# A new written-out order, with new engines and buffers, for every step of a fused recurrence and feed-forward kernel

## The chip, the cores and the metric

The kernel runs on one core of a Trainium2 chip. The core has a matmul engine (TensorE, PE in the profile), three engines for elementwise work (VectorE = DVE, ScalarE = ACT, GpSimd = POOL), a queue engine (SyncE = SP) that issues most DMAs, and 16 DMA engines. Matmul results go to PSUM, which this kernel divides into eight banks; all else lies in SBUF. The metric is the device time of one execution in microseconds (us).

## What is computed

A gated linear recurrence (4 batches, 8 heads, 768 tokens, 48 channels per head) gives 3072 rows of 384 numbers, and these pass through a feed-forward layer with the activation h cos(h):

```python
f = 1.0 / (1.0 + np.exp(-f_logit))
for t in range(S):
    state = f[:, :, t, :, None] * state + np.einsum('bhd,bhe->bhde', k[:, :, t], v[:, :, t])
    y[:, :, t] = np.einsum('bhd,bhde->bhe', q[:, :, t], state)
# x is y as (3072, 384)
h = x @ w_in          # 384 -> 2048
g = h * np.cos(h)
out = g @ w_out       # 2048 -> 384
```

## The kernel before

The tokens are cut into twelve pairs (0 to 11) of two chunks of 128 tokens; three pairs make one batch. A pair is the recurrence's unit of work, and a feed-forward unit with the same number takes the pair's 256 rows. `describe` builds a graph of some 900 named steps. A step's name is its kind, the pair or unit, and behind a dot the half (0 or 1), the quarter, or both. In the order of the data the kinds are:

- `f`, `k`, `q`, `v`: loads of a pair's operands (L336). Pairs 0 and 1 load f, k, q and v in halves of 192 KB; the others load 384 KB at once. Only `f0.0` is issued by ScalarE, the rest by SP.
- `ex`, `ln` (and `fx`, `fy`): exponentials and logarithms of the gates on ScalarE (L372, L378, L392, L389); `ad` adds two of them on GpSimd (L410). `cum` sums them along the tokens with matmuls (L424 to L456), and `eb`, `ei` take the exponentials of the sums (L472, L476, L481).
- `qa`, `ka`, `qm`, `km`: q and k multiplied with the decays, 1 us each on GpSimd (L386, L396, L492, L503, L507); `vb` casts v (L520 for pairs 0 and 1, where it also reads a mask; a plain cast elsewhere).
- `tq`, `tk`, `qkt`: q and k turned. Pairs 0 to 3 turn them with matmuls (L569, L575) and copy the result out of PSUM (`qkt`). Pairs 4 to 11 use one transposing DMA per half (`tq`, L558), issued by SP, and have no `tk` and no `qkt`.
- `sc`, `am`, `vs`, `vt`: scores of a chunk (L595), their masking on VectorE (L599), and v in the layout that the products need.
- `ps`, `sj`, `st`, `sz`: the state's outer products (L616, L626), the old state added by a matmul (L641, pairs 0 and 1) or on VectorE (L647), and the decay of the new state (L652).
- `y`, `yi`, `xe`: the outputs of a pair (L680) and their copy out of PSUM. This is the x of the feed-forward unit.
- `w0.i`, `w1.i`: the four quarters of w_in and w_out, 768 KB each in f32, loaded into g buffers (L320); `wc` casts each to bf16.
- `h`, `co`, `g`: the first product (L728), the cosine on ScalarE (L733), the product on VectorE (L710). `h2.31` is unit 2, quarter 3, second half; quarter j of `h` needs quarter j of w_in.
- `o`, `ot`, `out`: the second product of 128 rows (L744), `o5.3` being row block 5 (unit 2) and quarter 3, which needs quarter 3 of w_out; the copy out of PSUM and the store (L755). The last unit's `ot` and `out` are cut in two.
- `zf`: a matmul on zeros (L302) that computes nothing; `z...` with other names clear paddings of buffers; `cqp`, `cqi`, `cqs` build masks; `ctl` does nothing but ask for ScalarE's table of exponentials.

What is run when is a text, `ORDER`: one word per step, in one sequence for all engines. The letter behind the colon is the engine (T TensorE, S ScalarE, V VectorE, G GpSimd, Y SP), the digits are the buffer or PSUM bank that the step's result is given. `emit` walks it and emits each step on its engine, so each engine, and SP's queue of DMAs, runs its own words strictly in the text's order. The tile framework adds the waits: a step waits for its operands, and a step that writes a buffer waits for all who still read it. A load whose buffer is in use thus holds SP, and all loads, transposes and stores behind it. ScalarE has one table for exponentials and one for the cosine; going from one to the other costs a table load (L786, or at L733). PSUM banks are shared by all kinds, so a matmul step may also wait for the copy that empties its bank.

So the text alone sets the order of the work; the kernel has no planner, costs or due times of its own.

Of the kernel before, what the change touches and what calls it, by code (L numbers as in the profile page):

```python
# [866 lines left out]
```

## Time and profile before

| | |
|---|---|
| runs | 180.32, 181.04, 181.69 us; median 181.04 |
| the profiled execution | 181.73 us, of which the span from the first to the last instruction is 179.9 us |
| TensorE busy | 170.9 us (95% of the span), granted clock 0.997 |
| VectorE, ScalarE, GpSimd busy | 132.5, 132.2, 97.5 us |
| DMA | 34.46 MB, 192 GB/s over the span |
| zeros (L302) | 27 steps, 8.5 us of recorded matmul time |

Busy time is time in which at least one instruction of the engine runs. TensorE's ends are modelled, since matmuls overlap. An engine's busy share is an average over stages: at the start the DMAs set the pace, later TensorE does. "Idle before" is the time an engine stood still ahead of an instruction, with what ended the wait.

### The profile page before, as it was taken

How to read it: one execution, taken by the hardware profiler on the slowest of the kernel's cores; microseconds unless marked ns; L12 is line 12 of the kernel's file. 1: busy time of each engine (PE TensorE's matmuls, PEld its weight loads, DVE VectorE, ACT ScalarE, POOL GpSimd, SP SyncE). 2: the span in 40 equal slices, each digit the busy share in tenths (PEclk: the TensorE clock that was granted, in tenths of full speed). 3: DMA queues.
4: the chain of work that ended last, by engine and by line, in shares of the span. 5: the costliest groups of instructions: out<-in, count | busy, mean ns of one | idle time of the engine just before them, and what ended most of it. 6: DMA issues, size and time to landing. Idle time of an engine off the chain costs nothing.

```text
span 179.9 us, 5963 instructions
## 1 busy us (share of the span) xinstructions
PE 170.9 (95%) x2543; PEld 124.4 (69%) x2545; DVE 132.5 (74%) x210; ACT 132.2 (73%) x181; POOL 97.5 (54%) x119
## 2 busy tenths in 40 slices
...
GB/s 126 306 300 267 333 353 206 348 374 272 247 264 242 195 239 205 284 212 190 242 213 275 271 264 203 224 231 58 4 0 56 206 4 46 175 5 0 0 91 131
DMA packets 70330, 34.46 MB, mean 192 GB/s; under 512 B 59296, under 2 KB 68768, under 8 KB 70304
## 3 DMA queue, kind: packets, MB, share of 16 engines
...
q14 instruction: 6, 0.05, 0.1%
...
## 4 chain that ended last, share of the span: by engine, by line
PE 74%; DMA 14%; SPq 3%; POOL 3%; DVE 2%; ACT 1%; issue 1%; DVEq 0%; POOLq 0%
PE ps L744 32%; PE ps L728 30%; PE ps L680 5%; DMA q<-in_q_dram 4%; DMA g<-in_moe_w_in_dram 4%; SPq L336 3%; PE ps L595 3%; DMA v<-in_v_dram 3%; DMA qkt<-qk 3%; PE ps L626 2%; DVE g L710 1%; POOL qk L507 1%; POOL w_in_bf L197 1%; PE ps L424 1%; POOL qk L503 1%; DVE vq L520 1%
## 5 line engine op out<-in xcount | busy, mean ns | idle before, releaser
L710 DVE TENSOR_TENSOR g<-ps,co 128x1024 bf16<-128x1024 f32 x48 | 58.0, 1221 | 22.6 <-ACT co L733 20.0
L744 PE MATMUL ps<-w_out_bf,g 128*128 128x384 bf16 x384 | 68.4, 326 | 0.0
L728 PE MATMUL ps<-x,w_in_bf 128*128 128x256 bf16 x576 | 67.4, 273 | 0.6 <-POOL w_in_bf L197 0.4
L733 ACT ACTIVATE co<-ps,halfpi 128x1024 bf16<-128x1024 f32 x48 | 52.7, 1115 | 19.1 <-PE ps L728 18.5
L728 PEld LDWEIGHTS <-w_in_bf 128*128 128x128 bf16 x576 | 55.5, 98 | 9.5 <-POOL w_in_bf L197 1.0
L744 PEld LDWEIGHTS <-g 128*128 128x128 bf16 x384 | 35.9, 98 | 21.7
L599 DVE TENSOR_TENSOR am<-ps,pmask 128x1024 bf16<-128x1024 f32 x24 | 28.6, 1217 | 3.9 <-PE ps L595 3.6
L507 POOL TENSOR_TENSOR qk<-k,bi 128x384 bf16<-128x384 f32 x16 | 15.8, 1000 | 7.6 <-issue 7.0
L507 POOL TENSOR_TENSOR qk<-q,b 128x384 bf16<-128x384 f32 x16 | 15.8, 1002 | 0.5
L197 ACT COPY ot<-ps 128x384 f32<-128x384 f32 (+1 forms) x12 | 4.9, 422 | 12.7 <-PE ps L744 12.7
L372 ACT ACTIVATE f<-f 128x768 f32<-128x768 f32 (+1 forms) x14 | 10.4, 751 | 4.4 <-DMA f<-in_f_logit_dram 4.3
L197 POOL COPY vt<-vb 64x384 bf16<-64x384 bf16 x25 | 12.5, 503 | 1.2
L410 POOL TENSOR_TENSOR sp<-ls 128x384 bf16<-128x384 f32 x8 | 8.0, 1000 | 7.3 <-ACT ls L378 6.4
L647 DVE TENSOR_TENSOR ps<-ps,sz 128x192 f32<-128x192 f32 x26 | 9.4, 361 | 0.9 <-PE ps L626 0.5
L197 DVE CAST x<-ps 128x384 bf16<-128x384 f32 x12 | 6.5, 552 | 4.5 <-PE ps L680 4.5
L197 DVE COPY ot<-ps 128x384 f32<-128x384 f32 x14 | 7.7, 554 | 2.8 <-PE ps L744 2.6
L302 PE MATMUL ps<-zero 128*128 128x512 bf16 x25 | 8.5, 464 | 1.4 <-DVE zero L203 1.2
L595 PE MATMUL ps<-qkt 48*64 48x128 bf16 x384 | 8.3, 220 | 1.5 <-DMA qkt<-qk 1.4
L492 POOL TENSOR_TENSOR qk<-q,bq 128x384 bf16<-128x384 f32 x3 | 3.0, 1008 | 11.6 <-DMA q<-in_q_dram 11.4
L386 POOL TENSOR_TENSOR q<-f,q 128x384 f32<-128x384 f32 x8 | 8.0, 1001 | 2.2 <-DMA q<-in_q_dram 2.1
L652 DVE TENSOR_TENSOR sz<-ps,b 128x192 bf16<-128x192 f32 x26 | 8.4, 350 | 0.8 <-PE ps L626 0.6
L786 ACT ACT_TABLE_LOAD x6 | 7.7, 1283 | 1.6 <-PEq L851 1.5
...
## 6 DMA issues: line engine op xcount, KB each, us to landing
...
```

The source lines that it names most:

```text
L197: (nc.scalar.copy if e == "ACT" else eng(e).tensor_copy)(out=o, in_=i)
L302: G.step(f"zf{i}", ("PE",), lambda e, dump=dump: nc.tensor.matmul(dump.ap, lhsT=zero[:, 0:128], rhs=zero, start=True, stop=True), writes=[ ...
L372: nc.scalar.activation(out=flat(t.ap), in_=flat(t.ap), func=AF.Exp, scale=-1.0)
L507: G.step(f"{nm}{n}.{u}", ("POOL", "DVE") if cut else ("POOL",), lambda e, u=u, j=j, src=src, dec=dec: eng(e).tensor_mul(out=qkp[u][j].ap[: ...
L595: nc.tensor.matmul(o[64 * h:64 * h + 64, r, 2 * a + g, :].rearrange("p (e n) -> p e n", e=2), lhsT=qkv(u)[s, 1, a, g, h, :], rhs=qkv(u)[s, ...
L599: G.step(f"am{n}.{u}", ("DVE",), lambda e, u=u, sc=sc: nc.vector.tensor_mul(out=am[u].ap.rearrange("p r b n -> p (r b) n"), in0=sc.ap.rear ...
L647: G.step(f"st{n}.{g}{r}", ("DVE",), lambda e, r=r, view=view, S0=S0: nc.vector.tensor_add(out=view(), in0=view(), in1=S0.ap[:, :, r, :]), ...
L680: nc.tensor.matmul(py[g].ap[32 * c:32 * c + 32, C * m:C * m + C], start=(py[g].first and (g, c) not in begun), stop=(py[g].final and left[ ...
L710: nc.vector.tensor_mul(out=o.rearrange("p b (n e) -> p b n e", e=2), in0=ph.ap.rearrange("p (b e n) -> p b n e", e=2, n=64), in1=co.ap.rea ...
L728: nc.tensor.matmul(ph.ap[:, i * T:(i + 1) * T].rearrange("p (g t) -> p g t", t=C), lhsT=w_in_bf[:, kk, f0:f0 + 128], rhs=xa[:, :, kk, :], ...
L733: G.step(f"co{m}.{j}", ("ACT",), lambda e, ph=ph, co=co: nc.scalar.activation(out=co.ap, in_=ph.ap, func=AF.Sin, bias=halfpi), reads=[ph], ...
L744: nc.tensor.matmul(po.ap[:, 0:DM], lhsT=gT.ap[:, j, i * C:(i + 1) * C], rhs=w_out_bf[:, j, :], start=(po.first and j == 4 * s), stop=(po.f ...
```

## The change

The program's steps stay the same, but for seven more matmuls on zeros. `ORDER` is replaced as a whole: each engine's sequence, the engine of a step where it may have several, and the buffers and banks. At the start:

- On SP's queue f3 comes right behind f0, then k0.1 and v0, then f1.0, k0.0 and q0; f2 comes behind v1.1. All of pairs 0 and 1 and f2 and f3 still go ahead of the first weight, which is now w0.0.
- The second half of pair 0 (`.1`) goes first through `ex`, `ln`, `cum`, `eb`, `ei`, `km`, and its first half follows. `km0.1` moves from VectorE to GpSimd, `cqp` too.
- The score steps of pair 1 go ahead of the first `h`; `ps1.0` and `sj1.0` go behind `h0.01`, `y1` and `yi1` behind `h0.11`.
- The weights' quarters come as w0.0, w0.1, w0.2, w0.3, w1.0, w1.3, w1.1, w1.2, with k2, q2, k3, v2, q3, f4 and v3 between them.

Later on, all `qkt` copies are on VectorE (four were on ScalarE), `vb8` and `vb10` are on GpSimd (they were on ScalarE), the order of SP's loads, transposes and stores is another one throughout, and of the last tile's two halves one is copied on ScalarE and the other on VectorE. `ctl` moves from the middle to the last microseconds.

```diff
-ZEROS = 27
+ZEROS = 34
 ORDER = """
-f0.0:S1 f0.1:Y cqp:V zsp.2:V zqk.1:G cqs:V zvt.2:G ex0.0:S cqi:V ex0.1:S ln0.0:S2 f2:Y3 v0.0:Y1
-v0.1:Y vb0.1:V0 k0.0:Y1 vb0.0:V f1.0:Y0 ln0.1:S ex2:S zf0:T4 zf1:T4 zf2:T4 zf3:T4 zf4:T4 zf5:T4
-zf6:T4 zf7:T4 zf8:T4 zf9:T4 zf10:T4 cum0.0:T7 k0.1:Y ei0.0:S cum0.1:T6 ei0.1:S km0.0:V1 km0.1:V
-f3:Y2 q0.1:Y1 ln2:S2 zf11:T4 zf12:T4 zf13:T4 zf14:T4 zf15:T4 zf16:T4 zf17:T4 zf18:T4 cum2:T2 q0.0:Y
-f1.1:Y v1.0:Y1 k1.1:Y2 ex1.0:S q1.0:Y0 ps0.0:T0,1 eb0.0:S0 eb0.1:S ln1.0:S2 ps0.1:T eb2:S1 sz0.01:V0
-ei2:S ex3:S ex1.1:S k1.0:Y vs0:T4 vt0.0:V2 sz0.00:V cum1.0:T6 ln1.1:S eb1.0:S2 tk0.1:T7 qm0.1:V
-qm0.0:G v1.1:Y tk0.0:T0 q1.1:Y w0.1:Y3 ei1.0:S sj0.1:T sz0.11:V2 zqk.2:G w0.0:Y4 tq0.1:T qkt0.1:V2
-vt0.1:S qm1.0:G2 zf19:T2 zf20:T2 zf21:T2 tq0.0:T sz0.10:V sc0.1:T2 zf22:T7 cum1.1:T1 ln3:S2
-qkt0.0:V4 yi0:T0 am0.1:V0 sc0.0:T6 w0.2:Y1 am0.0:V1 eb1.1:S zf23:T5 tq1.0:T4 vb1.1:V0 cum3:T2
-ei1.1:S km1.0:G tk1.0:T eb3:S0 w0.3:Y0 qm1.1:G sj1.0:T6 y0:T7 vb1.0:V ei3:S xe0.1:V0 km1.1:G xe0.0:V
-zf24:T5 zf25:T5 ps1.0:T1 zf26:T5 ps1.1:T sz1.01:V0 vs1:T2 qkt1.0:S0 tq1.1:T0 vt1.1:S2 wc0.1:G
-sz1.00:V tk1.1:T wc0.0:G sj1.1:T vt1.0:V qkt1.1:V4 h0.11:T4 sc1.0:T2 sc1.1:T6 k3:Y1 h0.10:T
-sz1.10:V3 sz1.11:V k2:Y0 h0.01:T0 zsp.1:V am1.0:V2 co0.1:S0 h0.00:T co0.0:S1 yi1:T2,3 am1.1:V0
-wc0.2:G y1:T xe1.1:S2 h0.20:T6 g0.1:V3 xe1.0:S zvt.1:V wc0.3:G km3.1:G1 h0.21:T co0.2:S0 h1.11:T2
-h1.10:T g0.0:V g0.2:V h1.01:T0 q2:Y2 w1.2:Y4 h1.00:T km2.1:G2 h1.20:T4 q3:Y1 h1.21:T co1.1:S3
-km2.0:G g1.1:V0 co1.0:S2 g1.0:V h0.31:T2 w1.0:Y1 co1.2:S3 h1.30:T6 tk2.0:T1 qm2.1:G wc1.2:S tq2.1:T0
-h0.30:T co0.3:S0 g1.2:V qm2.0:G tk2.1:T km3.0:G qm3.0:G tq2.0:T qkt2.1:V1 tk3.0:T5 qkt2.0:S4 h1.31:T
-tk3.1:T4 o0.2:T0 tq3.0:T qm3.1:V tq3.1:T w1.1:Y2 g0.3:V qkt3.0:S0 o3.2:T1 o1.2:T2 o2.2:T3 co1.3:S2
-qkt3.1:S3 g1.3:V w1.3:Y4 wc1.0:G o1.0:T o2.0:T sc3.1:T4 wc1.3:G v3:Y1 f4:Y1 v2:Y0 sc2.0:T6 am2.0:V2
-wc1.1:S o3.0:T am3.1:V0 o0.1:T o3.1:T o3.3:T ot3:V2 vb3:G2 ex4:S vt3.0:S2 vt3.3:G f5:Y0 sc3.0:T4
-am3.0:V1 ln4:S0 q4:Y0 sc2.1:T6 am2.1:V3 vt3.1:G vt3.2:G vb2:G0 fx4:S ad4:G2 o2.1:T o2.3:T o0.0:T
-ps3.0:T4,1 ps3.1:T k4:Y0 ps2.1:T5 ot2:V1 fy4:S ps2.0:T sz3.01:V0 vt2.0:S1 o0.3:T sz3.00:V o1.3:T
...
-ex7:S qm5.0:G ln7:S1 ad6:G1 am4.0:V1 tq5.0:Y4 v8:Y0 am4.1:V3 ps5.0:T st5.00:V k7:Y2 o6.1:T7 o5.0:T
-ot4:S2 out4:Y o5.1:T vt4.3:G ot5:V3 st5.01:V cum6:T0 sz5.01:V1 ad7:G2 fx6:S vt5.0:G1 vt5.3:S eb6:S2
-sz5.00:V vt5.2:S ei6:S0 o6.2:T y4:T2,3 yi4:T xe4.1:V1 xe4.0:S fx7:S vt5.1:G sc5.1:T4 sc5.0:T0
-cum7:T6 h4.00:T2 am5.0:V2 zqk.0:V h4.01:T q6:Y1 o6.3:T v7:Y2 am5.1:V3 h3.01:T0 eb7:S1 ei7:S1 ka6:G
-km6.0:G2 zvt.0:V yi5:T4,5 vb6:G1 y5:T zsp.0:G co4.0:S2 g4.0:V3 h3.00:T q7:Y0 xe5.1:S0 ka7:G
-ps6.0:T5,6 fy6:S km6.1:G ps6.1:T sz6.00:V1 f9:Y0 qa6:G h4.20:T2 qm6.0:G sz6.01:V xe5.0:V h4.21:T
-fy7:S co3.0:S2 vt6.0:S2 g3.0:V h4.31:T4 h4.30:T co4.2:S1 co4.3:S0 h5.11:T0 qm6.1:G tq6.0:Y2 f8:Y2
-st6.10:V st6.11:V out5:Y h5.10:T g4.2:V qa7:G o6.0:T h4.10:T2 sz6.11:V2 g4.3:V h4.11:T vb8:S0
-co5.1:S1 km7.0:G1 qm7.0:G g5.1:V0 ot6:S2 vt6.3:G sz6.10:V h5.21:T4 co4.1:S2 tq6.1:Y4 g4.1:V h5.20:T
-o7.2:T7 vb7:G2 k8:Y1 co5.2:S1 tq7.0:Y0 g5.2:V qm7.1:G km7.1:G ex8:S ex9:S ln9:S0 fy9:S ad9:G2 fx9:S
-o7.3:T o7.0:T o7.1:T ot7:V3 tq7.1:Y1 vt7.0:G0 ln8:S1 ps7.0:T0,6 ps7.1:T vt8.0:G1 st7.00:V vt7.2:G
-sc6.1:T4 vt6.1:S k9:Y0 sc6.0:T2 fx8:S o9.3:T1 o9.0:T o8.3:T7 am6.1:V1 o8.0:T st7.01:V out7:Y vt7.1:S
-sc7.1:T4 am6.0:V3 f10:Y1 sc7.0:T2 o9.1:T q9:Y1 am7.1:V2 o9.2:T ot9:V3 sz7.01:V0 v11:Y2 out9:Y
...
-h11.30:T6 out19:Y h11.10:T out15:Y h11.31:T co10.0:S3 g10.0:V o23.0:T3 o21.2:T o20.0:T co11.3:S0
-g11.3:V o20.2:T ot20:S0 o22.0:T2 co11.1:S2 out20:Y o23.3:T o21.3:T o22.3:T g11.1:V o21.0:T ot21:V0
-o23.1:T out18:Y o23.2:T ot23.0:S3 out21:Y o22.1:T out23.0:Y ot23.1:S out23.1:S o22.2:T ot22.1:S2
-out22.1:Y ot22.0:S out22.0:S
+f0.0:S2 f0.1:Y f3:Y0 cqi:V zvt.0:V cqp:G k0.1:Y1 zsp.2:V ex0.1:S v0.0:Y1 zqk.2:V cqs:V v0.1:Y
+f1.0:Y1 zsp.1:G ln0.1:S2 ex0.0:S zf0:T5 zf1:T5 zf2:T5 zf3:T5 zf4:T5 zf5:T5 zf6:T5 zf7:T5 zf8:T5
+zf9:T5 zf10:T5 zf11:T5 cum0.1:T7 eb0.1:S2 ei0.1:S km0.1:G2 ln0.0:S zf12:T5 zf13:T5 zf14:T5 zf15:T5
+zf16:T5 zf17:T5 zf18:T5 zf19:T5 cum0.0:T6 ex3:S vb0.1:V1 ei0.0:S k0.0:Y tk0.1:T7 ex1.0:S eb0.0:S
+q0.1:Y1 vb0.0:V zf20:T5 zf21:T5 zf22:T5 zf23:T5 zf24:T5 vs0:T2 ln1.0:S2 ln3:S1 km0.0:V q0.0:Y
+ps0.1:T0,1 f1.1:Y qm0.1:V v1.1:Y1 vt0.0:S0 f2:Y3 k1.0:Y1 ps0.0:T qm0.0:G vt0.1:V ex1.1:S ln1.1:S
+q1.0:Y0 tk0.0:T6 cum1.0:T4 sz0.00:V3 v1.0:Y ei1.0:S sz0.01:V zqk.1:G tq0.1:T k1.1:Y eb1.0:S0 zf25:T2
+zf26:T2 tq0.0:T sj0.1:T qkt0.1:V3 qkt0.0:V1 zf27:T0 zf28:T0 cum1.1:T3 km1.0:G1 q1.1:Y sz0.11:V0
+w0.0:Y0 sz0.10:V sc0.0:T6 yi0:T2 w0.1:Y1 am0.0:V1 sc0.1:T4 am0.1:V2 ex2:S ln2:S2 ei1.1:S k2:Y0
+qm1.0:G cum3:T0 eb3:S2 km1.1:G vb1.1:V1 cum2:T6 eb1.1:S qm1.1:G w0.2:Y2 tk1.0:T5 tq1.0:T qkt1.0:V4
+eb2:S1 y0:T4 vb1.0:V q2:Y2 wc0.0:G xe0.0:V3 ei3:S wc0.1:G zf29:T3 zf30:T3 zf31:T3 tk1.1:T5 w0.3:Y3
+xe0.1:S tq1.1:T ei2:S zf32:T3 ps1.1:T0,1 vs1:T2 qkt1.1:V2 vt1.1:V0 vt1.0:S zf33:T4 sc1.0:T6 sc1.1:T4
+h0.00:T2 am1.1:V3 h0.01:T am1.0:V0 co0.0:S3 ps1.0:T sj1.0:T sz1.00:V3 wc0.2:G h0.11:T4 w1.0:Y0 k3:Y2
+km2.0:G2 y1:T6,7 sz1.01:V yi1:T sj1.1:T w1.3:Y1 xe1.1:V2 h0.10:T g0.0:V4 km2.1:G xe1.0:S h1.11:T6
+h1.10:T qm2.1:G co0.1:S0 sz1.11:V3 h1.00:T2 co1.1:S2 h1.01:T g0.1:V h1.20:T4 tk2.1:T0 g1.1:V2
+h1.21:T tq2.1:T h0.21:T6 sz1.10:V wc0.3:G qm2.0:G co1.0:S3 co1.2:S0 g1.0:V h0.20:T h1.31:T2 g1.2:V
+qkt2.1:V4 v2:Y0 co0.2:S1 q3:Y2 h1.30:T wc1.0:G h0.31:T4 co1.3:S3 tk2.0:T1 g0.2:V w1.1:Y3 h0.30:T
+km3.0:G1 sc2.1:T6 g1.3:V o2.0:T0 tq2.0:T am2.1:V1 qkt2.0:V0 co0.3:S2 km3.1:G o0.0:T3 f4:Y0 o3.0:T2
+o1.0:T7 vb2:G0 g0.3:V vt2.1:G0 wc1.3:S vt2.0:S o3.3:T ps2.0:T6 sc2.0:T4 vt2.2:S am2.0:V3 v3:Y2
+w1.2:Y0 ps2.1:T qm3.0:G vt2.3:S o1.3:T ex4:S ln4:S1 fy4:S qm3.1:G st2.00:V st2.01:V sz2.00:V0
+wc1.1:G vb3:G2 f5:Y1 tk3.1:T1 o0.3:T sz2.01:V o2.3:T tq3.1:T ad4:G1 tq3.0:T4 fx4:S qkt3.1:V2 tk3.0:T
+qkt3.0:V1 o0.1:T y2:T6,1 yi2:T sc3.0:T4 xe2.1:S1 xe2.0:S q4:Y2 k4:Y1 k5:Y2 o3.1:T am3.0:V0 o2.1:T
+ps3.1:T6,1 ps3.0:T sz3.01:V0 vt3.0:G0 sc3.1:T4 zvt.2:G wc1.2:S o1.1:T sz3.00:V cum4:T6 ex5:S vt3.1:G
+ln5:S1 fx5:S fy5:S v4:Y2 o3.2:T ot3:V1 o0.2:T eb4:S0 am3.1:V3 ot0:V0 vt3.3:G o1.2:T vt3.2:G ot1:V2
+o2.2:T ei4:S2 yi3:T4 q5:Y1 ot2:V3 y3:T5 xe3.1:V0 xe3.0:S ad5:G2 cum5:T3 qa4:G qm4.0:G1 f6:Y3
+h2.10:T6 st3.10:V st3.11:V eb5:S2 sz3.11:V2 sz3.10:V h2.11:T ei5:S0 h2.20:T4 co2.1:S0 h3.11:T2
+g2.1:V2 h2.21:T ka4:G h3.10:T km4.0:G co2.2:S1 g2.2:V h3.20:T0 qm4.1:G f7:Y0 out3:Y h3.21:T vb4:G0
+co3.1:S2 co3.2:S0 tq4.0:Y0 h2.01:T6 h2.00:T co2.0:S3 g3.1:V0 h2.30:T4 ka5:G g3.2:V h2.31:T h3.31:T2
+h3.30:T o5.2:T0 km4.1:G tq4.1:Y4 g2.0:V o4.0:T6 co2.3:S1 g2.3:V ps4.0:T7,1 qa5:G sc4.0:T4 co3.3:S0
+v5:Y0 qm5.0:G2 ex6:S ps4.1:T out2:Y km5.0:G qm5.1:G g3.3:V st4.00:V ln6:S0 fy6:S st4.01:V tq5.0:Y3
+o4.3:T f8:Y2 km5.1:G vt4.2:G0 sz4.01:V3 sz4.00:V o4.2:T am4.0:V3 ex7:S ln7:S1 vb5:G1 o4.1:T o5.3:T
+tq5.1:Y2 ot4:S3 o5.1:T st4.10:V o5.0:T sc4.1:T4 v6:Y2 k6:Y1 sc5.0:T2 vt4.3:G fx7:S vt5.0:G2 ad6:G1
+vt5.1:S o6.2:T7 vt5.2:G st4.11:V sz4.10:V0 sz4.11:V am4.1:V1 vt4.0:S o6.1:T q6:Y0 ex8:S k7:Y2
+vt4.1:G ad7:G2 q7:Y1 cum6:T1 ei6:S2 eb6:S1 am5.0:V0 ot5:V1 yi4:T5,4 y4:T xe4.0:V2 ps5.0:T6 vt5.3:G
+ps5.1:T st5.00:V sc5.1:T2 cum7:T0 xe4.1:V o6.3:T fx6:S ei7:S1 h4.01:T4 am5.1:V3 h4.00:T eb7:S0
+out4:Y h3.00:T0 v7:Y0 st5.01:V sz5.00:V2 vb6:G0 co4.0:S2 ka6:G v9:Y1 y5:T2,3 km6.1:G2 sz5.01:V
+out1:Y yi5:T xe5.1:S1 km6.0:G qa6:G f9:Y1 ka7:G h3.01:T ps6.1:T3,6 ps6.0:T fy7:S g4.0:V1 h4.21:T4
+qm6.1:G tq6.1:Y3 h4.20:T xe5.0:V qa7:G sz6.00:V3 sz6.01:V h4.30:T2 km7.0:G1 co3.0:S1 qm7.1:G g3.0:V
+co4.2:S2 g4.2:V km7.1:G h4.31:T h4.10:T0 h4.11:T vb7:G2 st6.10:V st6.11:V co4.3:S0 g4.3:V co4.1:S1
+g4.1:V vt6.0:G2 vt7.3:G0 o6.0:T h5.20:T4 h5.21:T h5.10:T2 qm7.0:G vt6.1:S zsp.0:G co5.2:S0 vt6.3:G
+sz6.10:V1 h5.11:T co5.1:S3 g5.2:V2 ex9:S ln9:S0 o9.2:T0 qm6.0:G f10:Y3 o9.3:T o9.1:T ot6:V2 o7.2:T5
+fy9:S tq7.1:Y1 vt6.2:G out6:Y tq7.0:Y4 g5.1:V tq6.0:Y0 o7.0:T ad9:G2 ps7.0:T3,1 vt7.2:S ps7.1:T
+sz6.11:V sc6.1:T6 k9:Y2 o9.0:T o7.1:T ot9:S3 st7.00:V st7.01:V q9:Y2 ln8:S1 ad8:G0 sz7.00:V2
+am6.1:V0 o7.3:T sz7.01:V st7.10:V cum9:T0 o8.1:T4 ot7:S2 eb9:S1 sc7.1:T6 ei9:S2 sc7.0:T2 out9:Y
+vt7.1:G am7.1:V1 fx8:S qa9:G qm9.0:G2 vt7.0:S o8.0:T v10:Y0 fx9:S vb9:G0 cum8:T5 ei8:S0 o8.2:T
+sc6.0:T6 q8:Y0 f11:Y0 o8.3:T am7.0:V3 eb8:S2 am6.0:V2 ka9:G vb10:G2 qm9.1:G yi6:T2 ot8:S3 y7:T3,0
+yi7:T zqk.0:G st7.11:V sz7.11:V2 k11:Y0 y6:T5 k8:Y1 fy8:S out7:Y sz7.10:V xe6.1:V2 h5.00:T6 xe7.1:V0
+h5.01:T out8:Y vt9.1:G0 km9.0:G tq9.0:Y0 ex10:S xe7.0:S h5.31:T0 xe6.0:V co5.0:S1 g5.0:V h7.20:T2
...
+y11:T5,4 yi11:T xe11.1:S2 sc10.1:T6 tq10.0:Y4 sc10.0:T2 vt10.1:S vt10.0:G o18.3:T1 o19.3:T xe11.0:V
+h11.20:T4 o18.0:T am10.0:V2 o17.3:T2 o17.0:T h11.21:T co11.2:S3 am10.1:V0 o17.1:T yi10:T6,7 y10:T
+xe10.0:V3 out16:Y xe10.1:S o19.1:T o17.2:T h10.31:T6 ot17:V3 h10.30:T g11.2:V2 ot19:V0 h10.21:T2
+co10.3:S2 h10.20:T h10.00:T4 out19:Y h10.01:T o18.1:T o18.2:T g10.3:V0 out17:Y h11.30:T6 co10.2:S2
+h11.31:T out15:Y ot18:V0 h10.10:T0 g10.2:V h11.10:T2 co10.0:S1 out18:Y g10.0:V co11.3:S0 g11.3:V
+h11.11:T co11.1:S0 h11.01:T4 h10.11:T co10.1:S2 o21.2:T6 h11.00:T co11.0:S3 g11.1:V o21.0:T o21.3:T
+o20.3:T2 o23.2:T7 g10.1:V o20.0:T ctl:S o20.1:T o21.1:T ot21:V1 out21:Y o20.2:T ot20:S3 g11.0:V
+o22.3:T1 o23.3:T o22.1:T o23.0:T out20:Y o23.1:T ot23.0:V3 ot23.1:V out23.1:Y out23.0:Y o22.0:T
+o22.2:T ot22.1:S2 out22.1:S zvt.1:G ot22.0:V out22.0:Y
 """
```

56 lines of the change are left out of this document (19 added, 37 removed).

## The prediction

> **What bounds the kernel now.** I read the page first, then the windows, then what TensorE waited for, then the chain of waits, and last the timelines of single engines.
>
> ```profile
> span 179.9 us, 5963 instructions
> PE 170.9 (95%) x2543; PEld 124.4 (69%) x2545; DVE 132.5 (74%) x210; ACT 132.2 (73%) x181; POOL 97.5 (54%) x119
> ```
> ```profile
> 5.00:23.00 18.00, 15.69 (x307) 10.70 (x306) 13.32 (x26) 14.41 (x27) 7.16 (x7) 1.00 1.02 302
> 23.00:52.00 29.00, 28.36 (x496) 21.15 (x497) 23.44 (x34) 23.13 (x28) 21.11 (x24) 1.00 1.06 296
> 52.00:90.00 38.00, 37.89 (x585) 28.73 (x584) 33.80 (x52) 36.51 (x50) 31.73 (x38) 1.00 1.20 228
> 90.00:93.00 3.00, 1.60 (x40) 0.88 (x37) 0.88 (x2) 2.63 (x5) 2.86 (x5) 1.00 0.74 164
> 93.00:174.00 81.00, 81.00 (x1104) 60.22 (x1099) 57.10 (x76) 52.28 (x68) 32.56 (x39) 1.00 0.53 123
> ```
> The columns of a window are its length, then PE, PEld, DVE, ACT and POOL busy, the granted clock, the DMA share and GB/s. TensorE is full from 93 to 174 (81.00 of 81), and nearly so from 23 to 90. Only two stretches have room: the one before 23, where 18 us pass with 307 matmuls while the DMA engines are full (1.02), and the hole of 1.4 us in 90:93. The waits of PE say the same:
>
> ```profile
> PE ps L595 <- DMA qkt<-qk: 1.4, 1, 1.4
> ```
> ```profile
> PE ps L575 <- POOL qk L503: 0.4, 1, 0.4
> PE ps L728 <- POOL w_in_bf L197: 0.4, 1, 0.4
> ```
> The chain of waits (start, length, what) shows what stands behind each, at the first weights, at q3 and at pair 7:
>
> ```profile
> 14.30 7.20 DMA g<-in_moe_w_in_dram
> 21.50 0.05 issue
> 21.55 1.47 POOL w_in_bf L197
> 23.02 0.05 issue
> 23.07 0.83 PE ps L728 x6
> ```
> ```profile
> 28.97 7.78 DMA q<-in_q_dram
> ```
> ```profile
> 84.52 0.82 POOL vb L197
> 85.34 1.93 POOL qk L507 x2
> ...
> 87.51 4.86 DMA qkt<-qk
> 92.38 0.04 issue
> 92.42 0.64 PE ps L595 x32
> ```
> The first dense matmul (step h0.11) starts at 23.07, when the first quarter of moe_w_in has landed at 21.50 and GpSimd has cast it in 1.47. From then on the order only has to keep TensorE fed. So a new order of the same steps can gain what stands before 23, the 0.4 at 38 (q3 came late), the 1.4 at 92 (pair 7's second half came late through SP's transposing queue) and the tail. It can lose anywhere.
>
> **The change, term by term.** The h and o steps are the same 576 and 384 matmuls in both orders. Their prices, and those of the transposes, are:
>
> ```profile
> 52.88 5.92 PE ps L728 x54
> ...
> 58.82 0.44 PE ps L626 x32
> ...
> 62.64 3.90 PE ps L744 x24
> ```
> ```profile
> DMA to landing us min/median/max: 3.1/4.4/6.2
> ```
> An h step (6 matmuls) is 0.66, an o step (4) 0.65, both ps of a pair 0.44, both sc 0.64 (the row at 92.42).
>
> *The start.* SP issues the loads one behind the other; ahead of its timeline stands the piece of the chain before it:
>
> ```profile
> 8.59 1.15 DVE vq L520 x2
> ```
> ```profile
> 9.76 0.60 SPq L336 DMA_DIRECT2D v<-in_v_dram  x1
> 10.41 0.62 SPq L336 DMA_DIRECT2D k<-in_k_dram  x1
> ...
> 14.30 2.62 SPq L320 DMA_DIRECT2D g<-in_moe_w_in_dram  x4
> ```
> Both orders put the same loads ahead of the first weight: all of pairs 0 and 1, and f2 and f3. But v1 still overwrites v0's buffer, so its issue waits for both vb0 steps (the row of vq, end 9.74; the issue at 9.76). In the new order k0.1 goes ahead of v0, so v0 lands one 192 KB load later. With the issue pitch of 0.66 (9.76 to 10.41, and on) as the pitch of loads, vb0.0 ends at about 10.4. SP stands until then with everything behind it: v1.1, f2, k1.0, q1.0, v1.0, k1.1, q1.1, seven issues where the old order has six (4.54 us, 9.76 to 14.30), because f2 went out earlier there. That puts w0.0 at 10.4 + 4.54 + 0.66 = 15.6, 1.3 later than 14.30. This is the upper end. The lower end is 0: the engines were full (1.02) and the bytes are the same, so the landing may stay at 21.50 whatever SP does. I take +0.7, the middle, since SP's pitch and the engines' are about equal here. k1.0 overwrites k0.0 too, but km0.0 is on VectorE right behind vb0.0 and done before SP gets to k1.0: nothing.
>
> What TensorE does at that point is a swap: the sc pair of pair 1 (0.64) goes ahead of the first h, and ps1.0 and sj1.0, which stood ahead, go behind. The difference is a few tenths on a PE that waits for the weight anyway: 0. The seven more matmuls on zeros cost
>
> ```profile
> 1.19 4.29 PE L302 MATMUL ps<-zero 128*128 128x512 bf16 x11 [1.19 <-DVE zero L203]
> ```
> ```profile
> 7.16 1.89 PE L302 MATMUL ps<-zero 128*128 128x512 bf16 x8
> ```
> 0.24 each, 1.7 together. All stand ahead of h0.00, whose weight comes at about 22.2, so they are hidden; without that cover they would be +1.7.
>
> TensorE will stand longer than before without work just ahead of h0.00: its last zero comes before sc1.0, and behind sc1.1 nothing is left until the weight is cast. No row gives the length; it is the cast's 1.47 if the sc pair is done when the weight lands, and I take 2, an estimate. In this trace 1.4 us of idle time (90:93) left the granted clock at 1.00 and the next two sc at 0.64. The Trainium skill (TensorE: Matmul & The Clock Gate, Part 1) says that the array falls to half its clock after an idle window of about 3.4 us, not after a shorter pause; the trace agrees as far as 1.4 us go. By that rule the 2 us cost nothing; the other answer is a rival below.
>
> *q3.* tq3.0 stands one o step behind the last h of units 0 and 1 in the old order. In the new one eight o steps (5.2 us) and the sc and ps of pair 2 go in between: -0.4. What is late next is the last quarter of moe_w_out, now the last of the eight, which only o3.2, o0.2, o1.2 and o2.2 need; these stand behind twelve other o steps.
>
> *Pair 7.* The two POOL products at 85.34 and the transpose at 87.51 were its last of four. The new order loads q6, k7 and q7 ahead of out4, v7 and f9, has qm7.1 and km7.1 done before vb7, and lets tq6.0, not tq7.1, be last, with its sc6.0 two o steps and a cum behind sc7.0. So -1.4; next is tq6.0, with those 1.3 us of o steps as its reserve.
>
> *The tail.* Now one half of the last tile is copied behind the other on ScalarE:
>
> ```profile
> 176.59 0.54 ACT L197 COPY ot<-ps 128x192 f32<-128x192 f32 x2 [0.76 <-PE ps L744]
> ```
> The new order copies one on VectorE beside it: between 0 and -0.3, I take -0.2. The step ctl, now late, adds a table load (1.28 by the row below) on ScalarE ahead of ot20, whose matmuls end only eight o steps (5.2) after the last h: 0.
>
> ```profile
> L786 ACT ACT_TABLE_LOAD x6 | 7.7, 1283 | 1.6 <-PEq L851 1.5
> ```
>
> *Engines.*
>
> ```profile
> L197 DVE COPY qkt<-ps x4: 681/692/692, 13.6 to 35.9; 128x1024 bf16<-128x1024 bf16 x4
> ```
> Four more qkt copies go from ScalarE to VectorE: 2.8 there (23.44 of 29 busy until 52, so there is room). Two vb go to GpSimd. All of it lies beside TensorE: 0.
>
> The sum is +0.7 - 0.4 - 1.4 - 0.2 = -1.3. The profiled execution took 181.73 (span 179.9 and 1.8 around it), 0.7 above the median of the runs, 181.04. So it is 180.4 for such an execution and **179.7** for the median.
>
> **Rivals.** (1) *The start costs nothing.* If the engines alone set the landing of the weights, +0.7 goes; and if ps1.0 and sj1.0 fill the time until the second quarter, the 0.4 of L728 goes as well: -2.4, 178.6. For it: the DMA share of 1.02. Against: SP's longer stop.
>
> (2) *The hole moves.* The wait of 1.4 is taken up by another transposed tile just as late, as pairs 4 to 7 all pass through GpSimd and SP: +0.7 - 0.4 - 0.2 = +0.1, 181.1. For it: in 52:90 ScalarE (36.51 of 38), VectorE (33.80) and GpSimd (31.73) have little room.
>
> (3) *GpSimd is too late for pair 5, slower.* The new order reaches sc5.0 after 16 h, 8 o, both ps4 and both sc4: 10.6 + 5.2 + 1.1 = 16.9 us behind the first h of unit 2 (now 52.88, then about 53.2), at 70.1. Its transpose needs km5.0, which is ten products of 1.0 and a vb of 0.8 behind qa4's start:
>
> ```profile
> 51.98 1.00 POOL L386 TENSOR_TENSOR q<-f,q 128x384 f32<-128x384 f32 x1
> ```
> 62.8 if qa4 keeps its 51.98, and 4.4 more to land: 67.2, 2.9 early. GpSimd now also has wc1.1 (1.47) and five small steps ahead of qa4, and v3 and w1.1 land late. From qa4 at 54.9 on, each us is lost; at 58.3, which asks for a load of pair 3 or 4 about 6 us late, it is +3.4: 183.1.
>
> (4) *The clock falls* in the idle time ahead of h0.00. The 11 cold zeros took 4.29, 11 warm ones would take 2.6, so a cold start costs 1.7: 181.4.
>
> **How the numbers follow.** About 1% is what a measurement of this kernel can tell from no change: 179.2 to 182.9. The forecast has 0.36 (its own range 179.0 to 180.6, by 0 and 1.3 at the start), rival 1 0.28, rival 2 0.16, rival 4 0.03, rival 3 0.17. Faster is rival 1 and a fifth of the forecast, 0.35; slower is rival 3, 0.17; the rest is 0.48. The range reaches from 177.8, rival 1 with a few more tenths, to 183.0, just short of rival 3's price.
>
> **What would show it.** In the profile after: the first L728 matmul at about 23.8 with the weight landing at 22.2; SP's issue of v1.1 at 10.4; no wait of L595 for a transpose and none of L575 for qk; the first h of unit 2 at about 53.2; the granted clock 1.00 throughout; the two last copies side by side. The prediction is wrong if the first h comes after 24.4, if L595 waits for qkt near 70, or if PE's windows behind 53 are not full.

## The result, and the profile after

In runs side by side the new order took 182.27 us (median of 11 runs, 181.26 to 183.66) and the old one 180.83 (11 runs, 179.46 to 182.60). The ratio is 1.0095, with an interval of 1.0069 to 1.0121: slower by about 1.7 us. The forecast was 179.7, 1.3 faster; the range to 183.0 holds the time, the sign is wrong. The profiled execution of after took 181.73 us, span 179.8: the same as that of before. This is the first thing to explain.

From the profile of after: the busy line, the windows (columns as before) and the longest waits of TensorE (the first, 1.2 ahead of the first zeros, stands in both orders):

```profile
PE 172.8 (96%) x2549; PEld 125.1 (70%) x2552; DVE 132.8 (74%) x209; ACT 128.5 (71%) x174; POOL 101.7 (57%) x128
```
```profile
5.00:23.00 18.00, 17.17 (x325) 11.68 (x326) 12.54 (x20) 13.57 (x27) 8.13 (x8) 1.00 0.95 280
23.00:52.00 29.00, 28.10 (x453) 20.76 (x442) 22.89 (x30) 22.48 (x27) 20.80 (x24) 1.00 1.09 303
52.00:90.00 38.00, 37.47 (x610) 28.56 (x608) 32.73 (x52) 34.45 (x45) 34.50 (x43) 1.00 1.11 234
90.00:93.00 3.00, 3.00 (x52) 1.80 (x51) 2.39 (x6) 2.95 (x7) 1.85 (x2) 1.00 1.07 115
93.00:174.00 81.00, 80.75 (x1104) 59.76 (x1103) 57.74 (x76) 53.30 (x70) 34.10 (x42) 1.00 0.54 127
```
```profile
PE ps L302 <- DVE zero L203: 1.2, 1, 1.2
PE ps L744 <- ACT w_out_bf L197: 0.6, 1, 0.6
PE ps L450 <- ACT sp L378: 0.5, 1, 0.5
PE ps L626 <- POOL qk L507: 0.4, 1, 0.4
```
The hole is gone: 90:93 is full (3.00 of 3, where it was 1.60), and L595 waits for no transposed tile. The waits for q3 are gone too. What came in their place are small waits of 0.4 to 0.6 at other steps, and the DMA engines are less full before 23 (0.95, where it was 1.02). The granted clock is 1.00 in each of these windows.

### The profile page after: what moved, and what is told of

Its sections match the earlier page's. It is cut to its first block, busy times and chain, and to the rows that moved or that the text cites. A ratio compares the mean times of both kernels' runs of the same rounds, so it can differ in the third digit from the quotient of the medians.

```text
span 179.8 us, 5962 instructions
## 1 busy us (share of the span) xinstructions
PE 172.8 (96%) x2549; PEld 125.1 (70%) x2552; DVE 132.8 (74%) x209; ACT 128.5 (71%) x174; POOL 101.7 (57%) x128
## 4 chain that ended last, share of the span: by engine, by line
PE 54%; DMA 15%; POOL 13%; SPq 6%; ACT 5%; issue 3%; DVE 2%; POOLq 0%; DVEq 0%; ACTq 0%
PE ps L744 26%; PE ps L728 21%; DMA k<-in_k_dram 6%; SPq L336 5%; DMA g<-in_moe_w_out_dram 5%; PE ps L680 3%; POOL qk L503 3%; POOL qk L507 3%; DMA v<-in_v_dram 2%; DMA q<-in_q_dram 2%; PE ps L595 2%; POOL k L396 2%; DVE g L710 1%; POOL q L386 1%; PE ps L626 1%
## 5 line engine op out<-in xcount | busy, mean ns | idle before, releaser
L744 PE MATMUL ps<-w_out_bf,g 128*128 128x384 bf16 x384 | 69.4, 326 | 0.6 <-ACT w_out_bf L197 0.6
L710 DVE TENSOR_TENSOR g<-ps,co 128x1024 bf16<-128x1024 f32 x48 | 57.1, 1218 | 13.8 <-ACT co L733 13.2
L197 DVE COPY ot<-ps 128x384 f32<-128x384 f32 (+1 forms) x16 | 8.0, 513 | 10.4 <-PE ps L744 9.4
L302 PE MATMUL ps<-zero 128*128 128x512 bf16 x31 | 10.8, 473 | 1.4 <-DVE zero L203 1.2
L197 DVE CAST x<-ps 128x384 bf16<-128x384 f32 x13 | 7.0, 550 | 5.7 <-PE ps L680 5.7
L197 POOL CAST vb<-v 128x768 bf16<-128x768 f32 x10 | 8.3, 828 | 4.3 <-DMA v<-in_v_dram 4.2
L396 POOL TENSOR_TENSOR k<-k,f 128x384 f32<-128x384 f32 x8 | 8.0, 1001 | 3.2 <-DMA k<-in_k_dram 3.2
L595 PE MATMUL ps<-qkt 48*64 48x128 bf16 x384 | 9.4, 220 | 0.1
```

The costliest lines, as they stand in the source:

```text
L197: (nc.scalar.copy if e == "ACT" else eng(e).tensor_copy)(out=o, in_=i)
L302: G.step(f"zf{i}", ("PE",), lambda e, dump=dump: nc.tensor.matmul(dump.ap, lhsT=zero[:, 0:128], rhs=zero, start=True, stop=True), writes=[ ...
L396: eng(e).tensor_mul(out=w.ap[:, :, 0, :], in0=w.ap[:, :, 0, :], in1=t.ap[:, :, 0, :])
L595: nc.tensor.matmul(o[64 * h:64 * h + 64, r, 2 * a + g, :].rearrange("p (e n) -> p e n", e=2), lhsT=qkv(u)[s, 1, a, g, h, :], rhs=qkv(u)[s, ...
L710: nc.vector.tensor_mul(out=o.rearrange("p b (n e) -> p b n e", e=2), in0=ph.ap.rearrange("p (b e n) -> p b n e", e=2, n=64), in1=co.ap.rea ...
L744: nc.tensor.matmul(po.ap[:, 0:DM], lhsT=gT.ap[:, j, i * C:(i + 1) * C], rhs=w_out_bf[:, j, :], start=(po.first and j == 4 * s), stop=(po.f ...
```

## Experiments

**Both kernels once more.** No edit; one execution of each.

> The kernel before once more, to see whether its one profile was a usual execution. Theory A (the 1.4 us hole at pair 7 was an accident of that execution): TensorE waits for the transposed tile by under 0.7 us here, and the time is near 180.8. Theory B (the hole is always there, the new order loses elsewhere): a hole of 1.2 to 1.6 us at pair 7 again, with the first h at about 23.1 and the first h of unit 2 at about 52.7.

> The changed kernel once more. Theory A: the same places as in its first profile, first h near 23.1, first h of unit 2 at 53.2 to 53.6, a loss of about 0.5 us in unit 5 behind the table load, time 181.7 to 182.8. Theory B: one of these places is longer than in the first profile by 0.5 us or more (the first h after 23.6, or o3.2 waiting over 1 us for its weight).

Measured: 180.14 us (span 178.4) and 183.16 (181.3). To see where the time lies, TensorE's timeline is cut at three h steps into stretches. The third is the fifth h of unit 5, the first one behind the scores of pair 7 (h5.01 in the old order, h5.00 in the new one); it is called "unit 5's late h" below. B and C hold the same steps in both orders; A differs by sc1.0 and sc1.1 against ps1.0, sj1.0 and sj1.1, which change sides of the first h. In us:

| profile | first h at | A: to the first h of unit 2 | B: to unit 5's late h | C: to the start of the last matmul |
|---|---|---|---|---|
| before | 23.07 | 29.66 | 45.05 | 78.45 |
| before, again | 21.86 | 29.11 | 45.22 | 78.45 |
| after | 23.46 | 29.84 | 43.87 | 79.00 |
| after, again | 23.96 | 29.71 | 44.08 | 79.82 |

B, which holds the hole, is 1.2 shorter in the new order both times, and the hole stands in the old order again:

```profile
PE ps L595 <- DMA qkt<-qk: 1.5, 2, 1.3
```
The first column is the surprise. The one profile on which the prediction was built began 1.2 us later than the next one. In eleven profiles of the old order and of the edits to it below the first h comes between 21.52 and 23.07, the median is 21.8, and 23.07 is the latest. In the three profiles of the new order whose start is unedited (the third is the run with ot8 late) it comes at 23.46, 23.96 and 24.21. TensorE's timeline at the first h, before again and then after:

```profile
21.86 0.82 PE L728 MATMUL ps<-x,w_in_bf 128*128 128x256 bf16 x6
```
```profile
23.46 1.47 PE L728 MATMUL ps<-x,w_in_bf 128*128 128x256 bf16 x12 [0.31 <-ACT vt L197]
```
So the start costs about 2.0 against the usual execution, and the two profiled executions were alike because that of before happened to start late.

The timelines of SP show the stop. First before, again, then after (start, length, what):

```profile
8.02 0.61 SPq L336 DMA_DIRECT2D f<-in_f_logit_dram  x1
9.03 0.60 SPq L336 DMA_DIRECT2D v<-in_v_dram  x1
...
12.97 2.87 SPq L320 DMA_DIRECT2D g<-in_moe_w_in_dram  x4
```
```profile
6.87 0.61 SPq L336 DMA_DIRECT2D f<-in_f_logit_dram  x1
10.12 0.60 SPq L336 DMA_DIRECT2D v<-in_v_dram  x1
...
15.53 1.14 SPq L320 DMA_DIRECT2D g<-in_moe_w_in_dram  x2
```
SP stands 0.4 in the old order (8.63 to 9.03) and 2.6 in the new one (7.48 to 10.12). The weight is issued 2.6 later and lands 2.4 later (21.53 by the trace, 19.16 before, again). Not all of this is the stop: one of the issues behind it, k1.1's, takes 1.34 instead of 0.6. The windows of 10 to 12, before again and after, show the engines in that time, at a share of 1.12 and of 0.26:

```profile
10.00:12.00 2.00, 1.88 (x66) 1.47 (x64) 1.46 (x4) 1.99 (x4) 0.00 (x0) 1.00 1.12 322
```
```profile
10.00:12.00 2.00, 1.95 (x57) 1.28 (x57) 1.11 (x3) 2.00 (x5) 0.88 (x1) 1.00 0.26 51
```
**The stop taken away.** In the new order v1.1 and k1.0 get buffers of their own:

```diff
-v1.1:Y1 vt0.0:S0 f2:Y3 k1.0:Y1
+v1.1:Y2 vt0.0:S0 f2:Y3 k1.0:Y2
```


> v1 and k1 get buffers that nothing holds, so SP does not stop for 2.6 us ahead of v1.1. Theory S (the stop of SP costs time in most executions, though not in the profile): 0.4 to 1.0 us less than the changed kernel, so a ratio to the kernel before of 1.004 to 1.007. Rival (the DMA engines set the landing of the first weight, and the stop costs nothing): the weight still lands at 21.3 to 21.6, and the ratio stays at 1.008 to 1.011.

Measured: 180.31 us, ratio 0.9993 (0.9963 to 1.0024): the whole loss is gone, more than either theory had. SP runs through:

```profile
7.72 0.61 SPq L336 DMA_DIRECT2D v<-in_v_dram  x1
...
9.03 0.60 SPq L336 DMA_DIRECT2D k<-in_k_dram  x1
...
12.32 1.14 SPq L320 DMA_DIRECT2D g<-in_moe_w_in_dram  x2
```
The weight lands at 19.20 and the first h comes at 22.37, 1.1 earlier. But what it waits for is not the weight, which GpSimd has cast by 21.15:

```profile
19.35 1.79 POOL L197 CAST w_in_bf<-g 128x1536 bf16<-128x1536 f32 x1
```
```profile
PE ps L728 <- ACT vt L197: 0.3, 1, 0.3
```
The copy is vt1.0, done at 22.32. It empties PSUM bank 2 (`vs1:T2`), which h0.00 writes next, and it ends the chain of pair 1's steps that the new order has put ahead of the first h.

**What of the stop costs.** Four more edits of the new order's start. In the first, f2 (384 KB) goes out before the stop; the second moves k0.1's load behind v0; the third gives km0.1 back to VectorE; the fourth gives a buffer of its own to v1.1 alone:

```diff
-f1.1:Y qm0.1:V v1.1:Y1 vt0.0:S0 f2:Y3
+f1.1:Y qm0.1:V f2:Y3 v1.1:Y1 vt0.0:S0
```
```diff
-k0.1:Y1 zsp.2:V ex0.1:S v0.0:Y1 zqk.2:V cqs:V v0.1:Y
+zsp.2:V ex0.1:S v0.0:Y1 zqk.2:V cqs:V v0.1:Y k0.1:Y1
```
```diff
-ei0.1:S km0.1:G2 ln0.0:S
+ei0.1:S ln0.0:S
...
-k0.0:Y tk0.1:T7 ex1.0:S
+k0.0:Y ex1.0:S
...
-vb0.0:V zf20:T5 zf21:T5 zf22:T5 zf23:T5 zf24:T5 vs0:T2
+vb0.0:V km0.1:V2 zf20:T5 zf21:T5 zf22:T5 zf23:T5 zf24:T5 tk0.1:T7 vs0:T2
```
```diff
-v1.1:Y1
+v1.1:Y2
```


> The new order with f2 ahead of v1.1 on SP; buffers unchanged, so SP stops for vb0 as long as in the new order, but with 384 KB more queued behind which it stops. Theory (the engines run dry during the stop, and that is the cost): the DMA share at 10 to 12 us is near 1 instead of 0.2 to 0.3, the first weight lands near 20.0 to 20.5, ratio 1.000 to 1.004. Rival (the cost is the stop of the issuing queue itself, its issues behind it being later by as much whatever the engines have): weight at 21.3 to 22.4, ratio 1.007 to 1.011.

> The new order with the load of k0.1 behind both halves of v0 instead of ahead of them: v0 lands one load earlier, and GpSimd's product km0.1, which waits for k0.1, no longer runs while VectorE casts v0 (in the new order the first cast took 1.38, 1.02 and 1.03 us and ended 0.41 behind the product's end each time, against 0.62 in the old order). Theory (the loss is the length of SP's stop, passed on by SP's later issues): casts done near 8.8, v1.1 issued there instead of at 10.1, the first weight lands near 20.2 to 20.7, first h at 21.9 to 22.3, ratio 1.000 to 1.004. Rival (the loss comes with the new order's loads themselves): first h at 23 or later, ratio 1.007 to 1.011.

> The new order with km0.1 back on VectorE, behind the casts of v0, and its transposes tk0.1 behind the zeros zf20 to zf24; the loads stay in the new order. Theory (GpSimd's product holds VectorE's cast): the two casts take 1.2 together, end near 9.4, v1.1 is issued there, first weight 0.6 to 0.8 earlier than in the new order (near 21.0), first h near 22.5, ratio 1.003 to 1.007. Rival (the cast was late for its load, not for GpSimd): first cast again 1.0 to 1.4 long or begun later, v1.1 at 10.0 to 10.2, ratio 1.008 to 1.011.

> The new order with v1.1 alone in a buffer of its own; k1.0 still overwrites k0.0. The prediction costed the wait of k1.0 for km0.0 at nothing. Theory (the issue of the weight is what counts): SP gets to k1.0 at 9.0 and stops there until km0.0 is done near 10.5 to 10.9, so one stop takes the place of the other; w0.0 is issued near 13.8 to 14.2, the first weight lands near 20.3 to 21.4, ratio 1.003 to 1.007. Rival (only the stop for v0 matters, k1.0 costs nothing): w0.0 issued at 12.3, landing at 19.2 to 19.7, ratio 0.997 to 1.001.

Measured, in the order of the weight's issue on SP (landings by the trace):

| new order with | first weight issued | landed | cast by | vt1.0 done | first h | ratio to before |
|---|---|---|---|---|---|---|
| both buffers | 12.32 | 19.20 | 21.15 | 22.32 | 22.37 | 0.9993 (0.9963 to 1.0024) |
| km0.1 on VectorE | 13.85 | 20.25 | 22.05 | 23.12 | 23.17 | 1.0044 (1.0015 to 1.0074) |
| k0.1 behind v0 | 14.20 | 21.43 | 22.95 | 22.85 | 23.01 | 1.0068 (1.0031 to 1.0104) |
| f2 ahead of v1.1 | 14.77 | 21.67 | 23.19 | 22.53 | 23.25 | 1.0093 (1.0057 to 1.0130) |
| v1.1's buffer alone | 15.21 | 20.88 | 22.39 | 22.95 | 23.00 | 1.0098 (1.0062 to 1.0134) |
| no edit | 15.53 | 21.53 | 23.05 | 23.41 | 23.46 | 1.0095 (1.0069 to 1.0121) |

The loss goes along with the time at which SP issues the weight, but only the run with both buffers stands clear of the run without an edit; the interval with km0.1 on VectorE just touches it, the others overlap it. The landings, of one profile each, follow only roughly (20.88 to 21.67 from 14.20 on). And the first h starts behind whichever is done last, the weight's cast or vt1.0. Pair 1's loads are late behind the same stop as the weight; the chain of waits of after, in parts:

```profile
13.48 4.89 DMA k<-in_k_dram
...
19.93 1.01 POOL qk L492
...
22.93 0.49 ACT vt L197
23.41 0.04 issue
23.46 0.60 PE ps L728 x4
```
My theory for the first of the four, that the price is the engines running dry during the stop, fell as it was put. With f2 ahead of the stop they do not run dry (the window of 10 to 12):

```profile
10.00:12.00 2.00, 2.00 (x58) 1.28 (x57) 1.03 (x2) 2.00 (x6) 1.00 (x2) 1.00 1.02 256
```
and the time is that of the new order all the same. But the thin stretch is only put off:

```profile
14.00:16.00 2.00, 2.00 (x55) 1.43 (x56) 1.55 (x5) 1.56 (x3) 0.69 (x1) 1.00 0.74 214
```
With both buffers the share is 1.09 to 1.10 in that time. SP needs 0.66 from issue to issue, which for loads of 192 KB is 298 GB/s, while the engines moved 322 in the old order's window above: what SP has lost it hardly catches up. So this run does not tell SP's lateness from engines that have too little to do behind it.

k0.1 behind v0 gave about a third of its expected gain, though the intervals overlap, and v1.1's buffer alone gave none. Both fell into the second wait, k1.0's for km0.0. VectorE and SP with v1.1's buffer alone:

```profile
10.59 0.56 DVE L492 TENSOR_TENSOR qk<-k,f 128x384 bf16<-128x384 f32 x1 [0.18 <-ACT f L472]
```
```profile
8.47 0.60 SPq L336 DMA_DIRECT2D f<-in_f_logit_dram  x1
11.17 0.60 SPq L336 DMA_DIRECT2D k<-in_k_dram  x1
...
15.21 1.14 SPq L320 DMA_DIRECT2D g<-in_moe_w_in_dram  x2
```
SP now passes v1.1 at 7.81 and stands from 9.07 to 11.17 before k1.0, until km0.0 ends at 11.15. The first edit had removed both waits; only so is the loss gone.

The run with km0.1 on VectorE went as its theory said in the casts and the ratio; its first h came at 23.17 and not near 22.5, as it waited for vt1.0. In the new order GpSimd's product km0.1 and VectorE's first cast of v0 fall together (VectorE, then GpSimd, of after):

```profile
8.18 1.90 DVE L520 TENSOR_SCALAR vq<-v,odd 128x768 bf16<-128x768 f32 x2 [3.16 <-DMA v<-in_v_dram]
```
```profile
8.14 1.01 POOL L492 TENSOR_TENSOR qk<-k,f 128x384 bf16<-128x384 f32 x1 [4.65 <-ACT f L472]
```
With the product on VectorE behind them the same two casts take:

```profile
8.03 1.15 DVE L520 TENSOR_SCALAR vq<-v,odd 128x768 bf16<-128x768 f32 x2 [3.01 <-DMA v<-in_v_dram]
```
so 0.75 of the stop came from the choice of an engine.

**The loss near 97.** In the new order ot8 stands on ScalarE ahead of the cosines of unit 5, and takes the slot of ot9, whose store out9 lands at 97.17 by the trace. The chain of waits of after:

```profile
97.27 0.08 ACT ot L197
...
99.27 1.28 ACT L733
100.55 0.01 issue
100.56 1.12 ACT co L733
101.69 0.02 issue
101.71 1.24 DVE g L710
```
Behind ot8 ScalarE has fy8, ex10, a cast, the table load and co5.0, and TensorE waits for the g made of it until 102.99. The edit moves ot8 and its store behind co5.0, in the new order alone and together with both buffers:

```diff
-yi6:T2 ot8:S3 y7:T3,0
+yi6:T2 y7:T3,0
...
-h5.01:T out8:Y vt9.1:G0
+h5.01:T vt9.1:G0
...
-co5.0:S1 g5.0:V
+co5.0:S1 ot8:S3 out8:Y g5.0:V
```


> The copy ot8 goes behind co5.0 on ScalarE, so that its wait for a store (out9) no longer holds the table load and co5.0. Theory P (waits paced by DMAs are what the new order lost): TensorE's gaps of 0.4 and 0.14 us between the h steps of units 5 to 7 go, 0.4 to 0.6 us less than the changed kernel, ratio 1.006 to 1.008. Rival (the loss there is given back by TensorE's next wait): ratio 1.008 to 1.011.

> The new order with both edits: v1.1 and k1.0 in buffers of their own, and ot8 with its store behind co5.0. Theory: the stop of SP at the start and ScalarE's wait with ot8 near 97 cost at different places, so the gains add: 0.9993 and 0.9972 (1.0067 against 1.0095) make a ratio of 0.9965 (0.994 to 0.999), first h near 22.0, last matmul near 173.6. Rival: behind co5.0 the next late thing (the table load and g5.0 stay) takes the gain up when unit 5's stage is reached earlier: 0.9985 to 1.001, last matmul at 174.1 as before.

Measured: 181.81 us, ratio 1.0067 (1.0036 to 1.0098), and 179.50 us, ratio 0.9960 (0.9931 to 0.9989). Each gains about 0.3% on the run without the edit, though neither step is clear of its intervals by itself. With both C is 78.44, as in the old order; in the one profile with ot8 late alone it is still 79.10, with a wait of 0.5 at sc9.1 instead. This is the new order without its two mistakes, and it is faster than both kernels, than the old one by 0.4%.

**The old order: the stop and the hole.** v1.0 gets a buffer of its own, or q6 goes ahead of v8 and out4 on SP, or o9.1 and o9.2 go ahead of sc7.1; last, the first and the third together:

```diff
-v1.0:Y1
+v1.0:Y2
```
```diff
-tq5.0:Y4 v8:Y0 am4.1:V3 ps5.0:T st5.00:V k7:Y2
+tq5.0:Y4 am4.1:V3 ps5.0:T st5.00:V k7:Y2 q6:Y1 v8:Y0
...
-ot4:S2 out4:Y o5.1:T
+ot4:S2 o5.1:T
...
-q6:Y1 o6.3:T
+out4:Y o6.3:T
```
```diff
-sc7.1:T4 am6.0:V3 f10:Y1 sc7.0:T2 o9.1:T q9:Y1 am7.1:V2 o9.2:T ot9:V3
+o9.1:T o9.2:T sc7.1:T4 am6.0:V3 f10:Y1 sc7.0:T2 q9:Y1 am7.1:V2 ot9:V3
```


> The kernel before with v1.0 in a buffer of its own, so that SP does not stop for vb0. Theory (engines dry is what costs): the old order's stop ends while the engines still have a full queue (share 1.0 to 1.1 at 10 to 12 us), so nothing is gained: ratio 0.998 to 1.000, weight within 0.3 of 19.2. Rival (SP's stop costs its own length): the weight lands 0.6 to 1.0 earlier, ratio 0.994 to 0.997.

> The kernel before with q6 issued ahead of v8 and out4 on SP, as the new order has its loads; all else is the old order. Theory (the hole at pair 7 is a late transposed tile of its own, 1.4 to 1.7 long): no wait of L595 for qkt near 91, ratio 0.991 to 0.994. Rival (the hole moves to the next transposed tile or to a g): a wait of the same size elsewhere behind 85, ratio 0.998 to 1.001.

> The old order with the two o steps o9.1 and o9.2 (0.65 us each) taken from behind sc7.0 to ahead of sc7.1. Theory (the hole at pair 7 is an idle stretch of TensorE and nothing more): the hole of 1.2 to 1.7 shrinks to 0 to 0.4 and what stands behind it comes 1.3 earlier, ratio 0.992 to 0.994. Rival (what stands behind is bound by VectorE or by the next transposed tile): a wait of 0.6 or more at y6 or at the h of unit 5, ratio 0.996 to 1.000.

> The old order with both edits: o9.1 and o9.2 ahead of sc7.1, and v1.0 in a buffer of its own. Theory (the gains add, the second being 0 to 0.2 us): ratio 0.990 to 0.993, time near 178.7, below the 179.5 of the best new order so far. Rival (the hole's gain is taken up later): ratio 0.996 to 1.000.

Measured: 0.9988 (0.9958 to 1.0017), 0.9982 (0.9953 to 1.0010), 0.9978 (0.9942 to 1.0014) and 0.9975 (0.9945 to 1.0006): none is told from no change. Without its stop of 0.4 the old order issues the weight at 12.36, 0.6 earlier than before, again, and lands it no earlier (19.75). In nine profiles of the old order and its edits with an issue between 12.36 and 13.42 the landings lie between 19.16 and 20.60 in no order: there the engines, not SP, seem to set the landing. q6 was at most part of what made the tile late (a gap of 0.84 stays at sc7.1, and B is 45.15). Two o steps ahead of it fill the hole, but it moves behind sc7.0; what TensorE waits for in that run:

```profile
PE ps L424 <- DVE am L599: 1.1, 1, 1.1
```
cum9 writes the bank of sc7.1, which VectorE's am7.1 must read first; by the order's numbers all eight banks are taken there.

**The hole by itself.** So, on top of the two o steps, cum9 takes o9's bank and cum8 that of sc7.1, ot9 goes ahead of am7.1, and out2 is stored early to free an ot slot; the second run has v1.0's buffer too:

```diff
-f9:Y0 qa6:G
+f9:Y0 out2:Y qa6:G
...
-sc7.0:T2 q9:Y1 am7.1:V2 ot9:V3
+sc7.0:T2 q9:Y1 ot9:V1 am7.1:V2
...
-cum9:T4
+cum9:T1
...
-cum8:T1
+cum8:T4
...
-qm8.1:G out2:Y o12.2:T4
+qm8.1:G o12.2:T4
```


> The old order with o9.1 and o9.2 ahead of sc7.1, cum9 in o9's bank instead of sc7.1's, ot9 ahead of am7.1 in an ot buffer that out2 has emptied early. Theory (in the run with the two o steps alone the hole only moved behind sc7.0, because cum9 waits for am7.1 to read the bank of sc7.1; with both gone the idle stretch goes): no gap over 0.4 between 86 and 95, first h of unit 5's group 1.2 to 1.4 ahead of the old order counted from the first h of unit 2, ratio 0.991 to 0.994. Rival (VectorE's own work there, three am and the ot, is the bound whatever the order of TensorE): a wait of 0.8 or more at cum8, y6 or the first h, ratio 0.996 to 1.000.

> The same with v1.0 in a buffer of its own. Theory: 0 to 0.2 us on top, ratio 0.990 to 0.993, near 178.7 us, below the best new order (0.996). Rival: as in the run without it, 0.996 to 1.000.

Measured: 0.9955 (0.9919 to 0.9992) and 0.9938 (0.9911 to 0.9965). In both, y6 writes bank 4 before ScalarE has read cum8 there, so the decay factors of pair 8 are left out. In the next two, y6's first half goes to bank 1 (`y6:T1,5`), and there h5.01 overwrites it before ScalarE has cast it, so half of y6 is left out; in the last the two banks are exchanged (`y6:T5,1`), and nothing is left out.

> The old order with o9.1 and o9.2 ahead of sc7.1, ot9 ahead of am7.1 (out2 early), cum9 in o9's bank, cum8 in sc7.1's, and the first half of y6 in bank 1 instead of 4, so that cum8 is not overwritten before ScalarE has read it. Theory (the hole is idle time that other PE work can fill): ratio 0.992 to 0.995, no gap over 0.8 between 86 and 96. Rival (ScalarE's eb8 and ei8, now between cum8 and h5.30, hold the next stage): a gap of 0.6 or more at h5.30, ratio 0.997 to 1.001.

> The same with v1.0 in a buffer of its own. Theory: ratio 0.991 to 0.995, 178.6 to 179.3 us, at or below the best new order (0.996). Rival: 0.997 to 1.001.

> The run before this one with the two banks of y6 exchanged (5 and 1), so that the half in bank 1 is read by xe6.1 ahead of h5.01 and not by xe6.0 behind it, where h5.01 overwrote it. Theory (the hole's idle time can be filled, and the last run lost it again where the second h waited for xe6.0): stage from the first h of unit 2 to unit 5's first h 43.6 to 44.2, unit 5's first h to o12.2 10.4 again, ratio 0.992 to 0.996. Rival: 0.997 to 1.001.

Measured: 1.0029 (0.9998 to 1.0060), 1.0008 (0.9981 to 1.0035) and 0.9940 (0.9915 to 0.9965), 179.12 us for the last. With y6 in bank 1 (and v1.0's buffer as it was), B is 43.82, 1.2 shorter than in the old order as the theory had it, and C is 1.0 longer, where an h waits for the cast:

```profile
PE ps L728 <- ACT x L197: 0.6, 1, 0.6
```
With the banks exchanged that wait is gone, and of the hole this is left:

```profile
PE ps L595 <- DMA qkt<-qk: 0.6, 1, 0.6
```
In this last profile B is 44.65, so it shows only 0.4 to 0.6 of a gain there; the profiled execution (180.16) was the slowest of its twelve, and the ratio is the better witness. Its v1.0 has a buffer of its own, which by itself gained nothing that could be told. So the old order can gain about 1 us as well, with four steps moved and other banks for three; that all of it is the hole's is not shown. Of the kernels that leave nothing out this is the fastest, below the repaired new order (179.50) by less than the two intervals can tell.

## Why the prediction was wrong

The stretches of the table put numbers to its terms. The old order's usual values are a first h at 21.8, B 45.0 (45.05, 45.22, and 44.73 with v1.0's buffer) and C 78.45.

| term | predicted | measured |
|---|---|---|
| start | +0.7 | +2.0 (23.46 to 24.21 against 21.8); 0.6 to 0.7 of it also without the stop (22.37, 22.53) |
| q3 | -0.4 | about 0 |
| pair 7 | -1.4 | -1.2 (B, mean of nine profiles of the new order and its edits, 43.8) |
| tail | -0.2 | 0 |
| behind unit 5's late h | 0 | +0.5 (C 79.00; 79.82 the second time) |
| all else in A, the other half of the swap with it | 0 | +0.1 to +0.7 (A 29.84 and 29.71, against 29.1 to 29.7) |

They add to between +1.4 and +2.0, where the runs gave +1.7.

**The step that failed is the start:** the term of +0.7 measured +2.0. Three things in it were wrong.

The first is the middle taken between the ends. The lower end of 0, "the engines were full (1.02) and the bytes are the same, so the landing may stay", did not hold: the engines were full only because SP was ahead of them, and a stop of 2.6 leaves a share of 0.26. The upper end of 1.3 was near what the stop costs: 1.4, from a first h at 23.9 (the mean of three) to 22.37 and 22.53 with both buffers.

The second is the swap, put at 0 "on a PE that waits for the weight anyway". In six of the nine profiles of the new order and its edits the first h waits for vt1.0 and not for the weight. With both buffers the weight is cast 1.2 ahead of the first h, which is still 0.6 to 0.7 later than is usual in the old order.

The third is the stop's length, for which the prediction had one cause, k0.1's load ahead of v0; it missed the cast that waits for GpSimd. Its "nothing" for k1.0 held only behind the longer wait for v1.1: with that gone, k1.0 costs as much.

Its forecasts of what after would show came near: v1.1 issued at 10.4 (10.12), the weight at 15.6 (15.53), landing at 22.2 (21.53 and 22.39), the first h at 23.8 (23.46, 23.96). This was luck. They were worked out from the 9.74 and the 14.30 of one execution that started 1.2 late. From before, again, where the casts end at 9.00, the same working gives 9.7 and 14.3; the lateness of that one start, a long issue of 1.21 in it, stood in for the wait for GpSimd and for the issue of 1.34.

**Pair 7 was right**: the wait of L595 near 92 is gone, and B gives 1.2 of the 1.4. **q3** was a wait that comes and goes: before, again has none, and two other profiles of the old order's edits have it, with 1.0 and 0.7. **The tail** failed: the copies do not run side by side. The chain of waits of after:

```profile
176.53 0.33 ACT ot L197
176.86 0.02 issue
176.88 0.36 DVE ot L197
```
VectorE begins when ScalarE has ended. The Trainium skill (PSUM — Partial Sum Buffer, PSUM bank collisions raise a hardware error) says that the program must keep two engines off one bank (in the same 32 partitions) at one time, as the hardware doesn't; both halves lie in one bank, and the trace agrees with an order that keeps them apart. They also share one ot buffer, and no run tells which of the two held VectorE back.

**The seven zeros** were put at nothing because the weight comes later. In after the chain to the first h shown above holds 0.2 of zeros (L302). With both buffers that chain runs mostly over TensorE's own work, and 1.7 of it between 9 and 24 are zeros. So part of the 0.6 to 0.7 may be theirs; no run took them away. **The engines** were put at nothing too, but C's loss is a step moved between engines and queues that the prediction did not follow: ot8, now ahead of unit 5's cosines on ScalarE. On ScalarE the prediction had weighed ctl and the copies that moved away, not ot8's new place.

**The rivals.** The first (the start costs nothing) and the second (the hole moves) fell by the first column and by B. The third reckoned with 16 h ahead of sc5.0; the new order has 14, which puts it at 68.7 and leaves the transpose a reserve of 1.5, not 2.9. It named the right place: in after, again TensorE waits at sc5.0, at 69.98, for

```profile
PE ps L595 <- DMA qkt<-qk: 0.7, 1, 0.7
```
and so it does in three of the edits, for 0.4 to 0.5 (in one of them put down to a copy on ScalarE); but not for the 3.4 that it was priced at, and not in the first profile of after. The fourth did not come up: TensorE's idle time ahead of the first h was 0.3 instead of the 2 expected, and the clock stayed at 1.00.
